# Windowed attention feeding a split-precision SiLU MLP on one core: another order of the weight slices at the MLP's beginning, and the work between token groups put ahead of the rest, with its low parts on VectorE

## Chip, core and metric

One core of a Trainium2 chip runs the whole program in one launch. The metric is the time of one execution on the device in microseconds (us). The profile names the engines PE (TensorE matmuls; PEld are its weight loads), DVE (VectorE), ACT (ScalarE), POOL (GpSimd) and SP (SyncE, from whose queue every DMA of this kernel is issued). Each engine takes its instructions in the order in which the program emits them for it. [...]

## The reference, cut to what matters

```python
# q, k, v: (8 batches, 8 heads, 576 tokens, 64); causal window of 128, ALiBi slopes
scores = q @ k.T / 8 ; scores = where(mask, scores + bias, -1e9)
attn   = softmax(scores) @ v                    # per batch and head
x      = attn.transpose(0, 2, 1, 3).reshape(4608, 512)
h      = x @ w_in                               # w_in (512, 2048)
out    = (h * sigmoid(h)) @ w_out               # w_out (2048, 512), float32
```

## The kernel before, in words

**Tiles.** The 4608 tokens are 36 tiles of 128. Attention works on pairs p = 2i + q (tile i, four of the eight heads each, 72 pairs): `scores` (PE), `row_max` in two halves u (DVE, line 248), `exps` (ACT, 258), `p_hi` (ACT, 267), `p_lo` (DVE, 272), a transposing DMA (280), `attend` (PE, 318), `normalize` in two stages (DVE, 331 to 342), then x split in a high and a low half (ACT 352, DVE 358) and transposed by DMA (375). For each tile the values are split by `v_hi` (POOL, 199) and `v_lo` (DVE, 210). The first eight pairs take another way: transposes on PE (290), high and low parts out of PSUM (ACT 296, DVE 301), and `x_transpose` (PE 367, ACT 368, DVE 369) in four column blocks; their x must be there before the MLP can begin.

**MLP.** Nine groups g of 512 tokens, sixteen slices f of 128 hidden columns. Per slice `gemm1` (line 401, halves 0 and 1 with six products each) makes h in PSUM; then tanh on ACT (`act1`, 408), `act2` on DVE (413), the high part gh on ACT (`act3`, 419) and the low part gl on POOL (`act4`, 424); `gemm2` (436, two halves of six products) adds high*high, high*low and low*high into four PSUM banks. n = 16g + f numbers the slices. At a group's end four banks are stored (`store`, ACT 447 and DVE 445, DMA 448) through two buffers of the tag "io", and xh, xl, which have one buffer, are written for the next group by `x_parts` (ACT 388, POOL 389).

**Weights.** 32 slices ((f, 0) of w_in, (f, 1) of w_out) are loaded through two raw buffers of the tag "big", which the transposed x uses later too, and split in five steps (`w_split1` ACT 465, `w_shift` DVE 471, `w_low` DVE 476, `w_hi` ACT 486, `w_lo` DVE 490) spread over four positions. Some are split ahead of the MLP, the others one at every second position of group 0.

**Order.** All is written out by hand. A position is one half of a gemm; position 0 is the first gemm1 and attention's beginning has negative positions, from -82 on. `put(position, function)` hangs work on a position; `begin()` emits all of a position's work, then the gemm follows; `later(n, ...)` hangs work n positions on. A group has 64 positions: at 58 and 59 of a group stands the last slice's gemm1, at 60 and 61 gemm2 of slice 14, at 62 and 63 gemm2 of slice 15. In each group a pair's `scores` stand at position 58, its two `row_max` at 59 and 60, `v_hi` and `v_lo` of another tile at 60 and 61, and the `attend` that reads this v at 63; the next `scores` stand at 66. PSUM has eight banks: two (tag "a") serve scores, attend and small transposes from position 0 on, two hold h, four hold the outputs. An attend therefore needs a bank that a `row_max` has read, and the next scores need the bank that `normalize` of that attend has read.

The lines on which the prediction's steps rest:

```python
            later(1, act2, n)          # 645 to 647: every slice alike
            later(2, act3, n)
            later(2, act4, n)
            ...
            for i, x in enumerate([("g2", n - 1, 0), ("g2", n - 1, 1), ("g2", n, 0), ("g2", n, 1)]):
                if g + 1 < NG:
                    seq.append(("xt", g + 1, i))     # x_parts of tile i, one ahead of each gemm2 half
                seq.append(x)
```

Of the kernel before, what the change touches and what calls it, by code (L numbers as in the profile page):

```python
# [11 lines left out]
AF = mybir.ActivationFunctionType  # L12
ALU = mybir.AluOpType
# [17 lines left out]
NG = NT // TG  # L31
GT = TG // P
NF = DFF // P
NCC = DM // P
# [15 lines left out]
STEP = 8  # L50
# [2 lines left out]
LAST = [f"{kind}{f}" for f in range(NF - 1, NF - 5, -1) for kind in ("wih", "wil", "woh", "wol")]  # L53
WD = (1, 1, 2, 3)

CLOSE = (-4, 2, 8, 14, 20, 26, 32, 38)
W_EARLY = (-21, -17, -12, -8)


def at(p):  # L60

    if p < 2 * GT:
        return STEP * (p - 2 * GT) - 18
    if p < 4 * GT:
        return CLOSE[p - 2 * GT]
    return STEP * (p - 2 * GT) - LEAD
# [3 lines left out]
def tile_window_attention_then_silu_mlp(ctx, tc, qk, v, w_in, w_out, base8, out):  # L70
    nc = tc.nc
# [29 lines left out]
    xh = const.tile([P, NCC, TG], F32R, name="xh")  # L101
    xl = const.tile([P, NCC, TG], F32R, name="xl")

    def f32(ap):
        return ap.bitcast(F32)
# [4 lines left out]
    def next_tag(use):  # L110
        turn[use] = turn.get(use, -1) + 1
        return bank[use][turn[use] % len(bank[use])]
# [3 lines left out]
    def ps_of(tag, name):  # L116
        t = psum.tile([P, DM], F32, tag=tag, bufs=2 if tag in "ah" else 1, name=name)
        if tag == "a":
            spare["a"] = t
        return t  # L120

    def keep_warm(n):

        for _ in range(n):
            nc.tensor.matmul(
                spare["a"][:, 4 * (D + 1) :], ones16[:, :P], ones16[:, : DM - 4 * (D + 1)],
                start=True, stop=True, skip_group_check=True,
            )
# [52 lines left out]
    def block_of(i):  # L181
        return i % NBLK

    def load_k(i):
        ks[i] = pool.tile([P, NHP, P], F32, tag="k", bufs=KSLOTS, name=f"k{i}")
        nc.sync.dma_start(ks[i], qk[i, 1])

    def load_q(i):
        qs[i] = pool.tile([P, NHP, P], F32, tag="q", bufs=2, name=f"q{i}")
        nc.sync.dma_start(qs[i], qk[i, 0])  # L190
# [132 lines left out]
    xt, whole, now = {}, [], [0]  # L323
# [40 lines left out]
    def x_transpose(cc):  # L364
        xp = ps_of(next_tag("misc"), f"xp{cc}")
        for i in range(GT):
            nc.tensor.transpose(xp[:, i * P : (i + 1) * P], xt[i][:, cc * P : (cc + 1) * P], ident)
        nc.scalar.copy(xh[:, cc], xp)  # L368
        nc.vector.tensor_sub(xl[:, cc], xp, f32(xh[:, cc]))  # L369
# [12 lines left out]
            whole.remove(i)  # L382
            x_dma(i)

    def x_parts(i):
        t, first = xt[i & -2, "t"][:, i % 2], i % GT * P
        cols, scale = slice(first, first + P), vsc[i // NBLK][:, 1:2]
        nc.scalar.activation(xh[:, :, cols], t[:, :NCC], AF.Copy, scale=scale)  # L388
        nc.gpsimd.tensor_scalar(xl[:, :, cols], t[:, NCC:], scale, 1.0, op0=ALU.mult, op1=ALU.mult)  # L389

    hps, gact, ops = {}, {}, {}

# [18 lines left out]
    def act2(n):  # L411
        gt = gact[n]
        nc.vector.scalar_tensor_tensor(out=gt, in0=gt, scalar=1.0, in1=hps[n], op0=ALU.add, op1=ALU.mult)  # L413

    def act3(n):
        gt = gact[n]
        gh = pool.tile([P, TG], F32R, tag="gh", name=f"gh{n}")
        gl = pool.tile([P, TG], F32R, tag="gl", name=f"gl{n}")
        nc.scalar.copy(gh, gt)  # L419
        gact[n] = (gh, gl, gt)  # L420

    def act4(n):
        gh, gl, gt = gact[n]
        nc.gpsimd.tensor_sub(gl, gt, f32(gh))  # L424

    def gemm2(n, half):
        g, f = divmod(n, NF)
# [67 lines left out]
    def put(point, fn, *a):  # L495
        plan.setdefault(max(point, at(0)), []).append((fn, a))

    for p in range(NPAIR):
        i, q = divmod(p, 2)
        n = at(p)  # L500
        a = n + (2 * STEP + 2 if p < 2 * GT else 15 if p < 4 * GT else 13)
        put(n, scores, p)
        if block_of(i) in (SPLIT, SPLIT + 1):
            put(n + 1, other_batch, p)
        put(n + 1, row_max, p, 0)
        put(n + 2, row_max, p, 1)
        put(n + 2, exps, p, 0)
        put(n + 3, exps, p, 1)
        if p < 2 * GT:

            put(n + STEP + 1, p_transpose_first, p, 0)
            put(n + STEP + 1, p_hi_first, p, 0)
            put(n + STEP + 1, p_transpose_first, p, 1)
            put(n + STEP + 1, p_hi_first, p, 1)
            put(n + STEP + 3, p_lo_first, p, 0)
            put(n + STEP + 4, p_lo_first, p, 1)

            put(n + STEP + 1, keep_warm, 4)
            put(n + 2 * STEP + 2, keep_warm, 5)
        else:  # L520
            put(n + 3, p_hi, p, 0)
            put(n + 4, p_lo, p, 0)
            put(n + 4, p_hi, p, 1)
            put(n + 4, p_transpose, p, 0)
            put(n + 5, p_lo, p, 1)
            put(n + 5, p_transpose, p, 1)
        put(a + 0, attend, p)
        z = a + (3 if p < 2 * GT else 1)
        put(z, normalize, p, 0)
        put(z + 1, normalize, p, 1)  # L530
        put(z + 2, x_hi, p)
        put(z + 2, x_lo, p)
        if q == 0:
            if i > 1:
                put(at(2 * i - 3) + 1, load_q, i)
                put(at(2 * i - 3) + 1, load_k, i)
            if i >= GT:
                put(n - 2, load_v, i)
            put(a - 3, v_hi, i)
            put(a - 2, v_lo, i)  # L540
    for b in range(1, NBB):
        n = at(2 * NBLK * b)
# [8 lines left out]
    def later(n, fn, *a):  # L551
        put(pos[0] + n, fn, *a)

    wq = [(f, w) for f in range(NF) for w in range(2)]
    wi = [0, 0, 0]

    def w_next_load():
# [24 lines left out]
    with tc.manual_schedule():  # L582
        nc.gpsimd.memset(ones16, 1.0)
        nc.gpsimd.memset(ones, 1.0)
        make_identity(nc, ident)
        ps_of("a", "warm")
        keep_warm(16)

        warm = const.tile([P, 1], F32, name="warm")
        nc.scalar.activation(warm, ones[:, :1], AF.Exp)  # L590
        load_q(0)
        load_k(0)
        nc.sync.dma_start(tab[:, :, P:], base8[:, :, P:])
        for i in range(VCH):
            vscale_load(0, i)
        load_q(1)
        load_k(1)
        nc.sync.dma_start(tab[:, :, :P], base8[:, :, :P])
        nc.gpsimd.memset(v1[:, :, :, D : D + 1], 1.0)
        for i in range(VCH):  # L600
            put(at(0) + 3 + i // 2, vscale_reduce, 0, i)
        for x in range(3):
            put(at(0) + 8 + x, vscale_finish, 0, x)
        for n in range(2):
            put(at(0) + 14 + 8 * n, w_next_load)
        put(at(0) + 4, keep_warm, 10)
        put(at(0) + 6, keep_warm, 10)
        put(at(0) + 7, keep_warm, 6)
        for n in W_EARLY:
            put(n, w_next)  # L610
        for cc, n in enumerate((23, 24)):
            put(at(2 * GT - 2) + n, x_transpose, cc)
        while pos[0] < 0:
            begin()
            pos[0] += 1
        bank.update(scores=[("a", "a")])

        for g in range(NG):
            now[0] = g

            seq = []
            for f in range(NF):
                n = g * NF + f
                seq += [("g1", n, 0)] + [("xt", 0, 2), ("xt", 0, 3)] * (n == 0) + [("g1", n, 1)]
                if 0 < f < NF - 1:
                    seq += [("g2", n - 1, 0), ("g2", n - 1, 1)]
            n = g * NF + NF - 1
            for i, x in enumerate([("g2", n - 1, 0), ("g2", n - 1, 1), ("g2", n, 0), ("g2", n, 1)]):
                if g + 1 < NG:
                    seq.append(("xt", g + 1, i))  # L630
                seq.append(x)
            for k, n, half in seq:
                if k == "xt":
                    if n == 0:
                        x_transpose(half)
                    else:
                        x_parts(n * GT + half)
                    continue
                begin()
                x_send()  # L640
                if k == "g1":
                    gemm1(n, half)
                    if half == 1:
                        act1(n)
                        later(1, act2, n)
                        later(2, act3, n)
                        later(2, act4, n)
                else:
                    gemm2(n, half)
                    if n % NF == NF - 1:  # L650
                        store(g, 2 * half)
                        store(g, 2 * half + 1)
                if g == 0 and half == 0:
                    w_next()
                pos[0] += 1
        while plan:
            begin()
            pos[0] += 1
# [35 lines left out]
```

## Time and profile before

| what | value |
|---|---|
| median of 3 runs (lowest, highest) | 1046.36 us (1045.06, 1050.79) |
| the profiled execution's own time | 1045.97 us |
| its span, first to last instruction | 1044.2 us |
| busy: PE, DVE, ACT, POOL | 95%, 53%, 44%, 24% of the span |
| mean granted TensorE clock | 0.977 |

The prediction is worked against the profiled execution (1045.97 us). A share of the span says little here: DVE is at 53% on average, but close to full in the first 180 us, in which attention's beginning and all weight slices lie. The rows further down are therefore of single stretches: the beginning (0 to 81 us) and the turns between two groups, which follow each other every 109 us or so.

### The profile page before, as it was taken

How to read it: one execution, taken by the hardware profiler on the slowest of the kernel's cores; microseconds unless marked ns; L12 is line 12 of the kernel's file. 1: busy time of each engine (PE TensorE's matmuls, PEld its weight loads, DVE VectorE, ACT ScalarE, POOL GpSimd, SP SyncE). 2: the span in 40 equal slices, each digit the busy share in tenths (PEclk: the TensorE clock that was granted, in tenths of full speed). 3: DMA queues.
4: the chain of work that ended last, by engine and by line, in shares of the span. 5: the costliest groups of instructions: out<-in, count | busy, mean ns of one | idle time of the engine just before them, and what ended most of it. 6: DMA issues, size and time to landing. Idle time of an engine off the chain costs nothing. (4 is left out here: it accounts for less than half of the span.)

```text
span 1044.2 us, 16900 instructions
## 1 busy us (share of the span) xinstructions
PE 997.2 (95%) x6374; PEld 788.7 (76%) x6374; DVE 555.9 (53%) x1358; ACT 462.3 (44%) x968; POOL 248.5 (24%) x229
## 2 busy tenths in 40 slices
PE   7798898999999999999999999999999999999998
PEld 6676676777777776777777767776777767777886
DVE  5889987455545554545455545544455545542111
ACT  5666667333353445334344454434334454433222
POOL 3012222222222223222222222222222122223221
PEclk8899999999999999999999999999899999999999
DMA  7267977333453445333444445432434443221001
GB/s 232 85 186 191 253 206 191 92 84 78 72 112 81 105 111 139 81 62 81 121 82 81 101 104 131 100 71 65 106 76 74 86 111 79 59 37 51 1 1 40
DMA packets 201072, 104.91 MB, mean 100 GB/s; under 512 B 168224, under 2 KB 176416, under 8 KB 200992
## 3 DMA queue, kind: packets, MB, share of 16 engines
q1 hardware_dynamic: 200992, 103.84, 42.1%
q8 instruction: 50, 0.82, 0.3%
q14 instruction: 30, 0.25, 0.1%
HBM read 54.00 MB, written 9.44 MB: 61 GB/s over the span
## 5 line engine op out<-in xcount | busy, mean ns | idle before, releaser
L424 POOL TENSOR_TENSOR gl<-gt,gh 128x512 fp32r<-128x512 f32 x144 | 186.9, 1298 | 742.2 <-ACT gh L419 575.2
L408 ACT ACTIVATE gt<-h 128x512 f32<-128x512 f32 x144 | 85.9, 597 | 446.7 <-PE h L401 438.0
L436 PE MATMUL o<-woh,gh 128*128 128x512 f32 x576 | 232.4, 404 | 12.4 <-ACT gh L419 12.4
L401 PE MATMUL h<-xh,wih 128*128 128x512 f32 x576 | 238.8, 415 | 2.0 <-ACT xh L368 2.0
L413 DVE SCALAR_TENSOR_TENSOR gt<-gt,h 128x512 f32<-128x512 f32 x144 | 98.9, 686 | 264.8 <-ACT gt L408 264.8
L436 PE MATMUL o<-woh,gl 128*128 128x512 f32 x576 | 232.8, 404 | 5.1 <-POOL gl L424 5.0
L436 PE MATMUL o<-wol,gh 128*128 128x512 f32 x576 | 229.6, 399 | 0.0
L401 PE MATMUL h<-xl,wih 128*128 128x512 f32 x576 | 227.5, 395 | 0.2 <-DVE xl L369 0.2
L401 PE MATMUL h<-xh,wil 128*128 128x512 f32 x576 | 227.6, 395 | 0.0
L272 DVE SCALAR_TENSOR_TENSOR hr<-t,hr 128x512 f16<-128x512 f32 (+1 forms) x128 | 120.8, 944 | 82.8 <-ACT hr L267 82.4
L436 PEld LDWEIGHTS o<-woh,gh 128*128 128x128 f32 x576 | 109.9, 191 | 39.5 <-ACT gh L419 15.5
L436 PEld LDWEIGHTS o<-woh,gl 128*128 128x128 f32 x576 | 109.8, 191 | 36.3 <-POOL gl L424 10.3
L401 PEld LDWEIGHTS h<-xh,wih 128*128 128x128 f32 x576 | 109.0, 189 | 30.0 <-ACT xh L368 2.2
L436 PEld LDWEIGHTS o<-wol,gh 128*128 128x128 f32 x576 | 109.9, 191 | 25.8
L401 PEld LDWEIGHTS h<-xh,wil 128*128 128x128 f32 x576 | 108.8, 189 | 25.1
L401 PEld LDWEIGHTS h<-xl,wih 128*128 128x128 f32 x576 | 109.1, 189 | 20.5 <-DVE xl L369 0.5
L258 ACT ACTIVATE t<-t,mx 128x256 f32<-128x256 f32 (+1 forms) x288 | 120.5, 487 | 9.0 <-DVE mx L248 9.0
L419 ACT CAST gh<-gt 128x512 fp32r<-128x512 f32 x144 | 88.5, 614 | 53.3 <-DVE gt L413 52.4
L248 DVE CUSTOM_DVE_ANT_0 t<-sp,tab 128x256 f32<-128x256 f32 (+1 forms) x288 | 101.0, 404 | 15.2 <-PE sp L228 9.0
L358 DVE TENSOR_TENSOR x<-xs,x 128x256 f16<-128x256 f32 x64 | 73.1, 1143 | 45.5 <-ACT x L352 45.5
L228 PEld LDWEIGHTS sp<-k,q 64*128 64x128 f32 x1088 | 68.9, 192 | 25.7 <-issue 25.0
L228 PE MATMUL sp<-k,q 64*128 64x128 f32 x1088 | 83.4, 291 | 1.4 <-DVE xs L342 1.4
(68 smaller groups left out, 665.6 us busy)
## 6 DMA issues: line engine op xcount, KB each, us to landing
q<-qk SPq DMA_DIRECT2D x36, 256.0 KB, 3.0
k<-qk SPq DMA_DIRECT2D x36, 256.0 KB, 3.2
vm<-v SPq DMA_DIRECT2D x36, 256.0 KB, 3.7
out<-ot SPq DMA_DIRECT2D x36, 256.0 KB, 2.1
wr<-w_in SPq DMA_DIRECT2D x16, 512.0 KB, 3.9
wr<-w_out SPq DMA_DIRECT2D x16, 512.0 KB, 4.0
rv<-v SPq DMA_DIRECT2D x32, 256.0 KB, 3.0
hl<-hr SPq DMA_TRANSPOSE x128, 3.1
```

The source lines that it names most:

```text
L228: nc.tensor.matmul(sp[h][:, u, o], qs[i][rows, 2 * q + u], ks[i - 1 + o][rows, 2 * q + u], start=True, stop=True, skip_group_check=True,)
L248: nc.vector.tensor_tensor_reduce(out=t[:, h, 2 * P - n :], in0=st[p]["sp"][h][:, u, o].rearrange("p o c -> p (o c)"), in1=tab[:, 4 * q + 2 ...
L258: nc.scalar.activation(x, x, AF.Exp, bias=st[p]["mx"][:, 2 * u + h : 2 * u + h + 1], scale=-1.0)
L272: nc.vector.scalar_tensor_tensor(out=hr[:, 1], in0=t[:, :, 2 * P - n :], scalar=PSCALE, in1=hr[:, 0], op0=ALU.mult, op1=ALU.subtract)
L358: nc.vector.tensor_sub(xt[i][:, 1, cols], st[p]["x"], xt[i][:, 0, cols])
L401: nc.tensor.matmul(hps[n], w[:, cc], x, start=(half == 0 and i == 0), stop=(half == 1 and i == len(seq) - 1), skip_group_check=True,)
L408: nc.scalar.activation(gt, hps[n], AF.Tanh, scale=0.5 / W_SCALE)
L413: nc.vector.scalar_tensor_tensor(out=gt, in0=gt, scalar=1.0, in1=hps[n], op0=ALU.add, op1=ALU.mult)
L419: nc.scalar.copy(gh, gt)
L424: nc.gpsimd.tensor_sub(gl, gt, f32(gh))
L436: nc.tensor.matmul(ops[ti], a[:, t], w, start=(f == 0 and i == 0), stop=(f == NF - 1 and i == len(seq) - 1), skip_group_check=True,)
```

## The change

The weight slices come in the sequence (0,0), (1,0), (0,1), (2,0), (1,1), (3,0), (2,1), ... where it was (0,0), (0,1), (1,0), (1,1), ... Three are split ahead of position 0, at positions -72, -19 and -6; before, four were, at -21, -17, -12 and -8. The first two loads stand at -81 and -65, before at -68 and -60. Pair 8's scores move from position -4 to -1, with all that follows from them, its attend staying at 11. Pair 7's attend moves from -8 to -11, ahead of the first `x_transpose`, and loses the filler matmuls (`keep_warm`) in front of it; the other early pairs have theirs behind their attend. At a group's end `turn_over` emits act2, act3 and act4 of the last slice and x_parts of the next group's four tiles at once behind tanh, at position 59; gl of that slice and all xl are DVE's then, not POOL's.

```diff
-CLOSE = (-4, 2, 8, 14, 20, 26, 32, 38)
-W_EARLY = (-21, -17, -12, -8)
+CLOSE = (-1, 2, 8, 14, 20, 26, 32, 38)
...
-    def x_parts(i):
+    def x_parts(i, part):
...
-        nc.scalar.activation(xh[:, :, cols], t[:, :NCC], AF.Copy, scale=scale)
-        nc.gpsimd.tensor_scalar(xl[:, :, cols], t[:, NCC:], scale, 1.0, op0=ALU.mult, op1=ALU.mult)
+        if part == 0:
+            nc.scalar.activation(xh[:, :, cols], t[:, :NCC], AF.Copy, scale=scale)
+            return
+        nc.vector.tensor_scalar(xl[:, :, cols], t[:, NCC:], scale, 1.0, op0=ALU.mult, op1=ALU.mult)
...
-        nc.gpsimd.tensor_sub(gl, gt, f32(gh))
+        (nc.vector if n % NF == NF - 1 else nc.gpsimd).tensor_sub(gl, gt, f32(gh))
+
+    def turn_over(n):
+        i = (n // NF + 1) * GT
+        more = n // NF + 1 < NG
+        if more:
+            x_parts(i, 0)
+        act2(n)
+        act3(n)
+        act4(n)
+        if more:
+            x_parts(i, 1)
+            for k in range(1, GT):
+                x_parts(i + k, 0)
+                x_parts(i + k, 1)
...
-        a = n + (2 * STEP + 2 if p < 2 * GT else 15 if p < 4 * GT else 13)
+        if p == 2 * GT - 1:
+            a = n + 2 * STEP - 1
+        elif p == 2 * GT:
+            a = n + 12
+        else:
+            a = n + (2 * STEP + 2 if p < 2 * GT else 15 if p < 4 * GT else 13)
...
-            put(n + 2 * STEP + 2, keep_warm, 5)
...
-        put(a + 0, attend, p)
+        put(a, attend, p)
+        if p < 2 * GT - 1:
+            put(a, keep_warm, 5)
...
-    wq = [(f, w) for f in range(NF) for w in range(2)]
+    wq = [(0, 0)] + [a for f in range(1, NF) for a in ((f, 0), (f - 1, 1))] + [(NF - 1, 1)]
...
-            put(at(0) + 14 + 8 * n, w_next_load)
+            put(at(0) + 1 + 16 * n, w_next_load)
...
-        for n in W_EARLY:
+        for n in (at(0) + 10, -19, -6):
             put(n, w_next)
...
-            for i, x in enumerate([("g2", n - 1, 0), ("g2", n - 1, 1), ("g2", n, 0), ("g2", n, 1)]):
-                if g + 1 < NG:
-                    seq.append(("xt", g + 1, i))
-                seq.append(x)
+            seq += [("g2", n - 1, 0), ("g2", n - 1, 1), ("g2", n, 0), ("g2", n, 1)]
...
                         act1(n)
-                        later(1, act2, n)
-                        later(2, act3, n)
-                        later(2, act4, n)
+                        if n % NF == NF - 1:
+                            turn_over(n)
+                        else:
+                            later(1, act2, n)
+                            later(2, act3, n)
+                            later(2, act4, n)
```

## Rows read from the trace of the kernel before

**Rows 1.** The view of who waited for whom, PE alone, whole span: the engine, line and tile that waited and what released it; us in total, times, longest us.
```profile
PE o L436 <- ACT gh L419: 12.4, 7, 1.8
PE av L318 <- DVE mx L248: 9.1, 6, 3.0
PE xp L367 <- DVE x L342: 5.2, 1, 5.2
PE o L436 <- POOL gl L424: 5.0, 10, 0.6
```

**Rows 2.** The view by stretches (windows): a stretch, its length, busy us of each engine (PE, PEld, DVE, ACT, POOL) with the number of instructions, the granted TensorE clock, DMA share, GB/s. The second and the third turn between groups.
```profile
288.00:298.00 10.00, 7.58 (x47) 5.41 (x46) 3.57 (x5) 6.65 (x13) 3.67 (x5) 0.83 0.39 113
398.00:408.00 10.00, 7.58 (x53) 5.51 (x52) 3.83 (x6) 7.46 (x16) 3.87 (x5) 1.00 0.48 123
```

**Rows 3.** The timeline of PE at four turns (first 177, second 287, third 397, sixth 724): start us, us, instruction; in brackets the idle time before it and what ended it. In each turn the first row is the first product of gemm2 of slice 14 and the last row the scores at position 66; of the second turn also the first product of slice 15's gemm2.
```profile
177.21 0.40 PE L436 MATMUL o<-woh,gh 128*128 128x512 f32 x1
...
191.49 0.72 PE L228 MATMUL sp<-k,q 64*128 64x128 f32 x8
...
286.99 0.40 PE L436 MATMUL o<-woh,gh 128*128 128x512 f32 x1
...
291.75 0.50 PE L436 MATMUL o<-woh,gh 128*128 128x512 f32 x1 [1.79 <-ACT gh L419]
...
300.52 1.16 PE L228 MATMUL sp<-k,q 64*128 64x128 f32 x16
...
397.19 0.40 PE L436 MATMUL o<-woh,gh 128*128 128x512 f32 x1
...
409.38 1.19 PE L228 MATMUL sp<-k,q 64*128 64x128 f32 x16
...
724.31 0.40 PE L436 MATMUL o<-woh,gh 128*128 128x512 f32 x1
...
739.21 1.16 PE L228 MATMUL sp<-k,q 64*128 64x128 f32 x16
```

**Rows 4.** The timeline of ACT at the second turn: tanh, xh of the first tile, two exps, p_hi, gh.
```profile
287.25 0.60 ACT L408 ACTIVATE gt<-h 128x512 f32<-128x512 f32 x1 [4.61 <-PE h L401]
287.75 0.72 ACT L388 ACTIVATE xh<-xt,vsc 128x512 fp32r<-128x512 f16 x1
288.36 0.90 ACT L258 ACTIVATE t<-t,mx 128x256 f32<-128x256 f32 x2
...
290.57 0.62 ACT L267 ACTIVATE hr<-t 128x512 f16<-128x512 f32 x1
291.09 0.61 ACT L419 CAST gh<-gt 128x512 fp32r<-128x512 f32 x1
```

**Rows 5.** The timeline of DVE at the second turn: act2, v_lo, the last of the four stores, normalize's second stage.
```profile
287.88 0.69 DVE L413 SCALAR_TENSOR_TENSOR gt<-gt,h 128x512 f32<-128x512 f32 x1 [2.22 <-ACT gt L408]
288.49 1.10 DVE L210 SCALAR_TENSOR_TENSOR v<-rv,vsc,v 128x512 f16<-128x512 f32 x1
...
298.17 0.69 DVE L445 TENSOR_SCALAR ot<-o 128x512 f32<-128x512 f32 x1 [1.66 <-DMA out<-ot]
...
299.18 0.42 DVE L342 TENSOR_TENSOR xs<-av,r 128x256 f32<-128x256 f32 x1
```

**Rows 6.** Groups of instructions by line and shape, whole span: busy us, mean ns of one, idle time before them. The low part of a w_in slice; row_max over 256 columns.
```profile
L490 DVE TENSOR_TENSOR wil<-wm,wih 128x512 fp32r<-128x512 f32 x16 | 11.9, 741 | 1.5 <-ACT wih L486 1.4
L248 DVE CUSTOM_DVE_ANT_0 t<-sp,tab 128x256 f32<-128x256 f32 x256 | 93.6, 419 | 8.5 <-PE sp L228 8.5
```

**Rows 7.** The page's list of DMA issues: how many, KB each, median us from issue to landing.
```profile
out<-ot SPq DMA_DIRECT2D x36, 256.0 KB, 2.1
xt<-x SPq DMA_TRANSPOSE x32, 3.1
```

**Rows 8.** The timeline of SP ahead of the first turn: the four transposing DMAs of the next group's x.
```profile
171.77 5.49 SPq L375 DMA_TRANSPOSE xt<-x  x4
```

**Rows 9.** The timeline of DVE at the beginning: the first weight slice's shift; the low parts of pair 7; normalize of pair 7; the memset with which pair 8 begins; the two gaps behind it; the row_max that frees the bank for the attend at position 11.
```profile
40.46 0.43 DVE L471 TENSOR_SCALAR wm<-wm 128x512 int32<-128x512 int32 x1 [0.23 <-ACT wm L465]
...
44.90 1.28 DVE L301 SCALAR_TENSOR_TENSOR hl<-pt,hl 128x512 f16<-128x512 f32 x2
...
53.74 0.22 DVE L331 TENSOR_SCALAR r<-av,vsc 128x4 f32<-128x4 f32 x1 [0.78 <-PE av L318]
...
55.86 0.79 DVE L239 MEMSET sp<- 64x384 f32 x2 [0.78 <-PE sp L228]
...
59.27 0.69 DVE L272 SCALAR_TENSOR_TENSOR hr<-t,hr 128x512 f16<-128x512 f32 x1 [1.26 <-ACT hr L267]
60.80 1.29 DVE L369 TENSOR_TENSOR xl<-xp,xh 128x512 fp32r<-128x512 f32 x2 [0.84 <-ACT xh L368]
...
80.42 0.42 DVE L248 CUSTOM_DVE_ANT_0 t<-sp,tab 128x256 f32<-128x256 f32 x1
```

**Rows 10.** The timeline of PE at the beginning: the attend at position 11.
```profile
80.99 1.46 PE L318 MATMUL av<-v,hl 128*128 128x65 f16 x24 [2.96 <-DVE mx L248]
```

**Rows 11.** The timeline of ACT at the beginning: the second half of pair 1's exps.
```profile
15.35 0.69 ACT L258 ACTIVATE t<-t,mx 128x128 f32<-128x128 f32 x2 [0.76 <-DVE mx L248]
```

**Rows 12.** The view of the raw weights' tile, up to 40 us, in which two slices are loaded while the first inputs still come in: us from issue to landing.
```profile
DMA to landing us min/median/max: 6.7/7.0/7.3
```

**Rows 13.** Groups of instructions by line and shape, whole span: a store on DVE, which reads PSUM.
```profile
L445 DVE TENSOR_SCALAR ot<-o 128x512 f32<-128x512 f32 x18 | 12.4, 692 | 45.5 <-PE o L436 33.3 <-DMA out<-ot 12.2
```

More of the change, by code (lines that the diff above doesn't have):

```diff
@@ L608, in tile_window_attention_then_silu_mlp @@
         put(at(0) + 7, keep_warm, 6)
-        for n in W_EARLY:
+        for n in (at(0) + 10, -19, -6):
             put(n, w_next)
-        for cc, n in enumerate((23, 24)):
-            put(at(2 * GT - 2) + n, x_transpose, cc)
+        for cc in range(2):
+            put(at(2 * GT - 2) + 23 + cc, x_transpose, cc)
         while pos[0] < 0:
@@ L627, in tile_window_attention_then_silu_mlp @@
             n = g * NF + NF - 1
-            for i, x in enumerate([("g2", n - 1, 0), ("g2", n - 1, 1), ("g2", n, 0), ("g2", n, 1)]):
-                if g + 1 < NG:
-                    seq.append(("xt", g + 1, i))
-                seq.append(x)
+            seq += [("g2", n - 1, 0), ("g2", n - 1, 1), ("g2", n, 0), ("g2", n, 1)]
             for k, n, half in seq:
                 if k == "xt":
[L634 to L637, printed above, removed]
+                    x_transpose(half)
                     continue
```

## Prediction

> **What bounds the kernel now.** I read first who waits for whom on PE, since PE is busy nearly all the time: what it waits for is what can be won. Four entries carry nearly all of it [rows 1]: gh at seven places, row_max ahead of an attend (the two PSUM banks of tag "a"), once 5.2 us for pair 6's x, and gl at ten places. The stretches then show where: the seven gh waits stand one at each turn between groups, and the clock counts too. [...] From the first product of slice 14's gemm2 to the scores at position 66 the first turn takes 14.28 us, the second 13.53, the third 12.19, the sixth 14.90 [rows 3]. [...] I let the second stand for the fourth, fifth and seventh too; six turns are then 81.2 us. Within a turn PE does twelve products in 2.8 us: (291.75 - 1.79 - 0.40 - 286.99) / 11 = 0.234 each [rows 3].
>
> Why gh is late: tanh ends at 287.85, act2 at 288.57, but ACT does an xh, exps, an xh, exps and a p_hi before gh at 291.09 [rows 4, 5].
>
> **The turn after the change.** Zero is the first product of slice 14's gemm2. tanh 0.26 to 0.86, act2 0.89 to 1.58, gh right behind it 1.6 to 2.2 (xh of the first tile fits beside act2) [rows 4, 5]; gl on DVE like the low part of a weight, 0.74 [rows 6], 2.25 to 3.0. PE wants gh at 2.8 and gl two products later, 3.27: both waits go.
>
> What is late next stands behind gl in DVE's queue. Position 59 now emits act2, gl and four xl ahead of position 60's row_max and 61's v_lo; before, row_max came in front of act2, and v_lo right behind it. The attend at 63 needs both, v_lo for its values and row_max for its bank. An xl is a tensor_scalar from SBUF to SBUF of 512 columns; the trace has none on DVE. Its ends are the shift of a weight slice, 0.43 [rows 9], and a store out of PSUM, 0.69 [rows 13]; it is like the first in both its places, so I take 0.43 and keep 0.69 for the range. A next instruction starts 0.08 before the end of the one in front (288.49 against 287.88 + 0.69 [rows 5]): four xl take 1.4 and end at 4.3, row_max two of 0.42 [rows 6], at 0.35 each, 5.0. v_lo is between 0.69 (act2's size) and 1.10 (its row, beside POOL's work [rows 5]); POOL has nothing there in the new order, so I take 0.8. attend starts at 5.8. PE is ready for it after eighteen products, at 4.2: a new wait of 1.6.
>
> [...]
>
> From 5.8 PE needs 0.73 for the attend (half of 1.46 at the lower clock [rows 10]), 1.4 for six products and 2.8 for twelve: ready for the scores at 10.75. These need the bank that normalize frees, and normalize stands behind the last store, which waits for a store's DMA [rows 5]. That chain: ACT does three more xh behind gh (0.62 each), to 4.05, then exps to 4.8, the second exps from row_max's first result on to 5.7, p_hi to 6.25 (durations [rows 4]); p_lo 0.69 to 6.95. SP's queue has p_lo's transposing DMA in front of the stores: 1.37 for one issue (5.49 / 4 [rows 8]), 8.3; the second store's issue at 8.7 (0.4 for the first, my estimate); landed 2.1 later [rows 7], 10.85; last store and normalize take 1.43 (298.17 to 299.60 [rows 5]). Scores at 12.4. So the turn ends by the stores, not by PE, and the wait of 1.6 ahead of the attend is inside it, as is a fall of the clock behind that wait. A fall behind the second wait (10.75 to 12.4) would show: 1.34 (13.53 - 12.19 [rows 3]), one turn in four or five, 0.3 each; bounds 0 and 2.7.
>
> Six turns: 6 × 12.4 + 1.8 = 76.2 against 81.2: **-5.0**.
>
> **The first turn** differs. One slice fewer is split early, so the last one starts at 56, not 54, and x can be sent only at 59, not 57. On SP the four transposing DMAs then stand behind q and k of pair 20, which wait for the scores of 58. These end at -2.8; with 1.0 for q and k (estimate) x issues at -1.8, the fourth at 2.3 [rows 8], landed at 5.4 [rows 7]; its xl, row_max 6.5, then the small reduction for which a transpose on PE waits at 62, and exps, p_hi, p_lo to 9.1, transposing DMA 10.45, stores landed 13, scores at 14.4 against 14.28 [rows 3]; with a chance of a slow stretch **+0.6** (-1 to +3).
>
> **The last turn** has no attention and the last slice no x: gl on DVE comes in time. They have two of the ten gl waits, none over 0.6 [rows 1]: **-0.8**.
>
> **The beginning.** Before, DVE splits two slices from 40.46 on, and pair 7's low parts begin at 44.90 [rows 9]; pair 6's normalize stands behind them, which is PE's 5.2 us [rows 1]. After, only slice (1,0) is there: low parts at 42.9, pair 6's x at 45.0. attend of pair 7 now goes first, waiting some 2 us for these low parts. Then two blocks of x, each transposes 0.5, xh 0.6, xl 0.7 and handovers, 2.05 together; not overlapped, because pair 7's attend keeps one of the two banks until a normalize that stands behind both. That normalize begins at 49.2 instead of 53.74: 4.5 earlier. Behind it slice (0,1) costs 2.4 on DVE and ACT, so pair 8's memset comes at 52.4 instead of 55.86: 3.5 earlier. From it to the row_max at 80.42 DVE has the same instructions in another sequence, and 2.1 us of gaps [rows 9], of which I take 1.3 as closed, because other work now stands where they are. PE waits 2.96 us for this row_max [rows 10]; its own way there shortens more than DVE's, so DVE sets the end: 4.8 earlier. Weights: a w_out slice now has 6 positions from split to use, as each w_in slice had before, and no low part of a weight is in the list of PE's waits: 0; if that cover were gone, it would be DVE's next instruction that is waited for anyway.
>
> Slice (0,0) at -72 stands in front of pair 1's second exps in ACT's queue. Its load, issued near 9.8 behind the first inputs, takes about 6.7 [rows 12]: landed at 16.5, against exps at 15.35 [rows 11]. That delays DVE and ACT by up to 1.8; the filler matmuls on PE hide most: 0.3 taken. On SP its load goes ahead of q and k of tile 2, which pair 4 is the first to read: 0. Fillers behind the attend instead of in front: 0. Sum **-4.5** (bounds -7.5 and 0).
>
> From position 11 to 56 each position has what it had, one slice shifted: 0.
>
> **Sum:** -4.5 - 5.0 + 0.6 - 0.8 = -9.7 on 1045.97, 1036.3. The median of the runs is 0.4 above that execution, so 1036.5.
>
> [...]
>
> **Rivals.** *The stores don't bind*: if normalize is through by 10.75, only the attend's wait is left, and six turns take 64.5: -16.7, in all 1025. For it: SP's issues may be quicker than I add them up. Against: the last store waits for a DMA already now [rows 5]. 12%.
> *Slow low parts*: xl at 0.69 moves the chain by 1.0 to 13.4, the turns then lose 1.0 with their slow stretches: 1042.7. 12%.
> *A beginning without gain*: the early slice holds pair 1's exps for its full 1.8 and PE carries it on, and DVE, which is full from 40 to 81, eats the rest: 1041. 14%.
> *Slower*: the clock. [...] 8%.
>
> **Numbers.** Forecast 54%, its own range 1031 to 1042; most of it and the first rival are faster by over 0.5% (5.2 us, about what a measurement of this kernel tells from no change), of the third rival half: 70%. Within 0.5%: 22%. Slower: the clock, 8%. The range 1025 to 1044 leaves out the clock rival and half of the first.
>
> **What would show it.** Right: no gh wait and no gl wait at seven turns; in their place waits of about 1.6 of attends for DVE (row_max or v_lo) at six, a short wait of scores for normalize; xl near 0.43; no wait of 5.2 for pair 6's x; attend of position 11 near 76 us behind a longer wait. Wrong: attends at the turns without a wait, or turns above 13.5 us, or the attend of position 11 where it was.

## The result, and the profile after

The changed kernel takes 1052.13 us (median; 1046.22 to 1057.94) against 1046.84 (1041.60 to 1051.00): a ratio of 1.0055, 95% interval 1.0031 to 1.0079, so 3 to 8 us slower where 10 faster was forecast. Its profiled execution is the slowest of its runs, 1057.94 us (span 1056.1, granted clock 0.973); the stage sums below come from it and overstate the loss by the clock, by about 6 us.

Against the span of before it is 11.9 longer. By the starts on PE: -0.5 up to the first product of slice 14's gemm2 at the first turn (176.74 against 177.21); +2.9 in the first turn; +10.9 in the six others; -1.4 in the last turn and the last slice, where the waits for gl went.

The view of who waited for whom, PE alone (us in total, times, longest), answers to [rows 1]:

```profile
PE sp L227 <- DVE xs L341: 14.6, 7, 3.5
PE av L317 <- DVE mx L247: 13.2, 12, 2.9
PE vt L162 <- DVE vcol L158: 8.3, 2, 4.7
PE av L317 <- DVE v L209: 3.8, 6, 0.6
PE o L452 <- POOL gl L425: 1.8, 2, 1.5
```

The seven waits for gh are gone, as are those for gl at the turns. In their place stand scores waiting for normalize, and attends for row_max and then v_lo. PE's timeline at the first, second and third turn (start, us; in brackets the idle time before it) answers to [rows 3]:

```profile
176.74 0.40 PE L452 MATMUL o<-woh,gh 128*128 128x512 f32 x1
...
184.42 0.37 PE L162 MATMUL vt<-ident,vcol 128*1 128x128 f32 x1 [4.72 <-DVE vcol L158]
...
289.42 0.40 PE L452 MATMUL o<-woh,gh 128*128 128x512 f32 x1
...
294.45 0.28 PE L317 MATMUL av<-v,hl 128*128 128x65 f16 x4 [0.67 <-DVE mx L247]
295.37 0.76 PE L317 MATMUL av<-v,hl 128*128 128x64 f16 x20 [0.64 <-DVE v L209]
...
300.26 0.48 PE L227 MATMUL sp<-k,q 64*128 64x128 f32 x2
302.72 2.04 PE L227 MATMUL sp<-k,q 64*128 64x128 f32 x14 [1.97 <-DVE xs L341]
...
318.99 1.16 PE L227 MATMUL sp<-k,q 64*128 64x128 f32 x16
...
402.44 0.40 PE L452 MATMUL o<-woh,gh 128*128 128x512 f32 x1
...
417.33 1.13 PE L227 MATMUL sp<-k,q 64*128 64x128 f32 x14 [3.51 <-DVE xs L341]
```

At the second turn two scores fit into a free bank at 300.26, 10.84 from zero (the forecast had PE ready at 10.75); the others run at 302.72, 13.30 from zero. From there to the next scores at 318.99 it is 16.3, where before it was always 13.2. The stretches of the second turn (engines PE, PEld, DVE, ACT, POOL, then the clock) answer to [rows 2] and say why:

```profile
297.00:300.00 3.00, 3.00 (x15) 2.41 (x13) 0.69 (x2) 0.00 (x0) 0.00 (x0) 1.00 0.83 211
300.00:303.00 3.00, 1.03 (x6) 0.61 (x6) 1.36 (x4) 1.48 (x3) 0.00 (x0) 0.93 0.96 264
303.00:306.00 3.00, 3.00 (x17) 2.58 (x17) 2.46 (x9) 0.63 (x2) 1.15 (x1) 0.50 0.50 139
306.00:309.00 3.00, 3.00 (x8) 2.32 (x8) 0.68 (x4) 0.00 (x0) 0.13 (x1) 0.50 0.00 0
```

Taken in stretches of 1 us, the granted clock stands at 1.00 (986 of the first 1043 before, 987 of 1056 now) or at 0.50 (37 and 49), and between the two only where it changes. Through the attend's two waits it holds at 1.00 (293 to 297 us), and behind the wait of the scores it falls to 0.50. The turns of before lost clock too: besides the second, at 0.83 in [rows 2], the fourth to the seventh, whose stretches in the trace of before are these (columns as above):

```profile
506.00:516.00 10.00, 7.59 (x47) 5.41 (x46) 3.69 (x5) 6.67 (x14) 3.81 (x5) 0.83 0.37 105
616.00:626.00 10.00, 7.98 (x48) 5.48 (x47) 3.69 (x5) 7.72 (x16) 4.13 (x6) 0.83 0.47 146
725.00:735.00 10.00, 7.66 (x43) 5.46 (x42) 3.69 (x5) 6.37 (x13) 3.98 (x6) 0.73 0.38 110
837.00:847.00 10.00, 7.58 (x45) 5.39 (x45) 3.46 (x5) 6.54 (x13) 3.55 (x5) 0.83 0.37 101
```

So five of its six turns fell, and only the third kept 1.00. In the changed kernel it is again five of six: 0.50 from 303, 419, 528, 641 and 750 us on, and 1.00 from 847 to 870, at the seventh. DVE at the second turn of the changed kernel, answering to [rows 5]:

```profile
291.68 0.69 DVE L425 TENSOR_TENSOR gl<-gt,gh 128x512 fp32r<-128x512 f32 x1 [0.69 <-ACT gh L420]
292.29 1.67 DVE L390 TENSOR_SCALAR xl<-xt,vsc 128x512 fp32r<-128x512 f16 x4
...
294.56 0.75 DVE L209 SCALAR_TENSOR_TENSOR v<-rv,vsc,v 128x512 f16<-128x512 f32 x1
...
301.14 0.69 DVE L461 TENSOR_SCALAR ot<-o 128x512 f32<-128x512 f32 x1 [3.45 <-DMA out<-ot]
...
302.15 0.42 DVE L341 TENSOR_TENSOR xs<-av,r 128x256 f32<-128x256 f32 x1
```

The last store waits 3.45 for the DMA of the second one, which has the same buffer, and normalize stands behind it. SP, answering to [rows 8], the first turn's x and the second turn's p_lo and first two stores:

```profile
174.89 6.20 SPq L374 DMA_TRANSPOSE xt<-x  x4
...
296.52 1.23 SPq L279 DMA_TRANSPOSE hl<-hr  x1
297.84 1.01 SPq L464 DMA_DIRECT2D out<-ot  x2
```

The first turn has a wait of its own: x is sent from 174.89 on (171.77 before), the last xl on DVE is late by it, and row_max and the small reduction stand behind that xl. PE waits 4.72 for the reduction, the row at 184.42 above; from 184 to 190 us the granted clock is 0.50 to 0.51.

In the beginning, ACT (first) and DVE (second) answer to [rows 11] and [rows 9]:

```profile
17.07 0.67 ACT L481 ACTIVATE wm<-wr 128x512 f32<-128x512 f32 x1 [2.23 <-DMA wr<-w_in]
17.65 0.68 ACT L257 ACTIVATE t<-t,mx 128x128 f32<-128x128 f32 x2
```

```profile
18.24 1.49 DVE L492 SCALAR_TENSOR_TENSOR wm<-wr,wm 128x512 int32<-128x512 int32 x1
...
44.54 0.43 DVE L487 TENSOR_SCALAR wm<-wm 128x512 int32<-128x512 int32 x1 [0.25 <-ACT wm L481]
...
57.09 0.78 DVE L238 MEMSET sp<- 64x384 f32 x2 [0.15 <-issue]
...
80.08 0.42 DVE L247 CUSTOM_DVE_ANT_0 t<-sp,tab 128x256 f32<-128x256 f32 x1
```

Slice (0,0)'s split waits 2.23 for its load, and pair 1's second exps come at 17.65 (15.35 before). The first shift behind the early pairs comes 4.1 late; the row_max at 80.08 is 0.3 early, and with it the attend at position 11, at 80.66 on PE where it was 80.99 [rows 10]. From 20 to 26 us the granted clock was 1.00 before and 0.50 after (the stretches 12 to 20 and 20 to 26, before, then after):

```profile
12.00:20.00 8.00, 5.12 (x32) 4.28 (x33) 5.49 (x28) 4.15 (x15) 3.81 (x5) 0.57 0.86 277
20.00:26.00 6.00, 6.00 (x84) 5.54 (x82) 5.01 (x21) 3.76 (x10) 3.58 (x5) 1.00 0.30 89
```

```profile
12.00:20.00 8.00, 3.55 (x21) 2.65 (x21) 5.20 (x20) 3.71 (x12) 3.56 (x4) 0.53 0.88 273
20.00:26.00 6.00, 5.79 (x42) 4.72 (x43) 4.47 (x18) 2.76 (x7) 4.87 (x6) 0.50 0.31 90
```

### The profile page after: what moved, and what is told of

Its sections match the earlier page's. It is cut to its first block, busy times and chain, and to the rows that moved or that the text cites. A ratio compares the mean times of both kernels' runs of the same rounds, so it can differ in the third digit from the quotient of the medians.

```text
span 1056.1 us, 16874 instructions
## 1 busy us (share of the span) xinstructions
PE 1002.5 (95%) x6369; PEld 794.9 (75%) x6369; DVE 574.5 (54%) x1399; ACT 463.3 (44%) x968; POOL 219.0 (21%) x188
## 4 chain that ended last, share of the span: by engine, by line
PE 79%; DVE 9%; DMA 5%; ACT 3%; issue 3%; SPq 1%; POOL 0%; DVEq 0%; ACTq 0%; POOLq 0%
PE h L402 35%; PE o L452 32%; PE sp L227 7%; PE av L317 4%; DMA wr<-w_in 2%; DMA out<-ot 2%; DVE wm L492 1%; DVE xl L390 1%; DVE wm L487 1%; DVE hr L271 1%; DVE ot L461 1%; DMA vm<-v 1%; DVE t L247 1%; ACT t L257 1%; DVE gt L414 1%
## 5 line engine op out<-in xcount | busy, mean ns | idle before, releaser
L425 POOL TENSOR_TENSOR gl<-gt,gh 128x512 fp32r<-128x512 f32 x135 | 176.9, 1310 | 800.0 <-ACT gh L420 643.3
L402 PE MATMUL h<-xh,wih 128*128 128x512 f32 x576 | 242.6, 421 | 0.2 <-ACT xh L367 0.2
L402 PE MATMUL h<-xl,wih 128*128 128x512 f32 x576 | 230.6, 400 | 0.5 <-DVE xl L368 0.5
L452 PE MATMUL o<-woh,gl 128*128 128x512 f32 x576 | 229.3, 398 | 1.8 <-POOL gl L425 1.8
L402 PE MATMUL h<-xh,wil 128*128 128x512 f32 x576 | 230.3, 400 | 0.0
L271 DVE SCALAR_TENSOR_TENSOR hr<-t,hr 128x512 f16<-128x512 f32 (+1 forms) x128 | 121.1, 946 | 74.8 <-ACT hr L266 74.4
L402 PEld LDWEIGHTS h<-xh,wih 128*128 128x128 f32 x576 | 110.9, 193 | 29.1 <-issue 1.2
L452 PEld LDWEIGHTS o<-woh,gl 128*128 128x128 f32 x576 | 108.7, 189 | 28.8 <-POOL gl L425 2.9
L452 PEld LDWEIGHTS o<-woh,gh 128*128 128x128 f32 x576 | 109.1, 189 | 25.4 <-ACT gh L420 0.5
L227 PEld LDWEIGHTS sp<-k,q 64*128 64x128 f32 x1088 | 74.2, 199 | 41.2 <-issue 40.9
L227 PE MATMUL sp<-k,q 64*128 64x128 f32 x1088 | 89.9, 300 | 14.7 <-DVE xs L341 14.6
```

The costliest lines, as they stand in the source:

```text
L227: nc.tensor.matmul(sp[h][:, u, o], qs[i][rows, 2 * q + u], ks[i - 1 + o][rows, 2 * q + u], start=True, stop=True, skip_group_check=True,)
L271: nc.vector.scalar_tensor_tensor(out=hr[:, 1], in0=t[:, :, 2 * P - n :], scalar=PSCALE, in1=hr[:, 0], op0=ALU.mult, op1=ALU.subtract)
L402: nc.tensor.matmul(hps[n], w[:, cc], x, start=(half == 0 and i == 0), stop=(half == 1 and i == len(seq) - 1), skip_group_check=True,)
L425: (nc.vector if n % NF == NF - 1 else nc.gpsimd).tensor_sub(gl, gt, f32(gh))
L452: nc.tensor.matmul(ops[ti], a[:, t], w, start=(f == 0 and i == 0), stop=(f == NF - 1 and i == len(seq) - 1), skip_group_check=True,)
```

## The experiments

The theory after the result: *the loss is the turn's. The scores wait behind a store that waits for a DMA, and PE's idle wait is followed by a stretch at a granted clock of 0.50; the beginning gains some us and gives them back.* The rivals: the loss is the beginning's; the attend's waits are what costs; the clock falls for another reason than the wait; and the turns of before lose as much clock, so that only the later scores are left as the loss. The table gives, from the traces, the time from the first product of slice 14's gemm2 to the next pair's scores (position 74), for the first turn and turns two to seven.

| run | median, ratio to before (95%) | first | two to seven | sum of six |
|---|---|---|---|---|
| before | 1046.84 | 27.5 | 26.7 25.5 26.9 26.4 28.1 27.0 | 160.6 |
| changed | 1052.13, 1.0055 | 30.4 | 29.6 29.7 28.1 28.1 29.7 26.4 | 171.5 |
| start_only | 1045.90, 0.9994 (0.9970 to 1.0019) | 28.8 | 26.7 25.5 27.0 25.4 27.0 25.4 | 157.1 |
| turn_only | 1050.39, 1.0051 (1.0024 to 1.0077) | 27.3 | 26.5 29.1 29.5 26.5 29.7 26.4 | 167.8 |
| early_later | 1049.59, 1.0021 (0.9994 to 1.0048) | 30.4 | 29.6 27.3 26.4 28.1 28.4 28.0 | 167.8 |
| stores_late | 1037.15, 0.9913 (0.9888 to 0.9938) | 30.2 | 24.4 28.2 24.4 27.7 24.3 24.3 | 153.4 |
| xl_behind_v | 1055.98, 1.0087 (1.0057 to 1.0117) | 28.7 | 27.9 29.7 29.3 29.3 27.9 27.8 | 171.9 |
| both_moves | 1034.10, 0.9883 (0.9855 to 0.9912) | 27.2 | 24.2 27.8 24.3 27.7 24.2 24.2 | 152.4 |
| fillers_in_h | 1047.92, 1.0008 (0.9989 to 1.0028) | 31.6 | 26.5 27.8 26.4 26.5 26.4 26.4 | 160.1 |
| four_buffers | 1033.18, 0.9875 (0.9846 to 0.9904) | 30.1 | 24.1 28.5 24.3 24.1 24.1 24.1 | 149.1 |
| four_buffers_xl_behind | 1025.57, 0.9807 (0.9781 to 0.9832) | 26.7 | 23.3 29.0 23.5 23.2 23.2 23.2 | 145.3 |
| same_old_start | 1026.80, 0.9815 (0.9788 to 0.9842) | 24.3 | 23.2 28.3 23.2 23.3 23.2 23.2 | 144.5 |

**Half of the change alone.** `start_only` has the changed beginning and the turn of before; `turn_only` the other way round (the diff is the change's own, cut at the turn).

> Only the beginning of the change (order of the slices, early split of slice (0,0), pair 8 and pair 7 moved), turns between groups as before. Theory: the early slice's ACT step waits 2.2 us for its load ahead of pair 1's exps, and the lower clock lasts longer behind it, so all starts some 4 us late and the 4 us won between 40 and 81 us are eaten: first shift of a slice on DVE near 44.5 us, first product of slice 14's gemm2 within 1 us of 177; in all 1046 to 1049. Rival, the predicted one: the beginning gives 4.5, 1042.

> Only the turn of the change (x_parts, act2 to act4 at once, gl and xl on DVE), beginning as before. Theory: PE is ready for the scores at 10.8 us from the first product of slice 14's gemm2, they wait to 13.3 for normalize behind the last store, and the clock falls behind this wait: next scores at 28 to 29.6 instead of 25.5 to 28.1; the whole loss lies here: 1050 to 1054. Rival: the loss is the beginning's and the turns are level or gain 5: 1042 to 1047.

The turn alone is as slow as the whole change, 1.0051 against 1.0055; the beginning alone gives nothing that can be told. The rival that the beginning is the loss falls. In start_only the first product at the first turn came at 173.9, not within 1 us of 177: the beginning had gained 3.3 there, and the first turn took 1.3 of it back.

**The early slice.**

```diff
-        for n in (at(0) + 10, -19, -6):
+        for n in (-58, -19, -6):
```

> The changed kernel, with slice (0,0) split at position -58 instead of -72, where its load has long landed. Theory: no wait of ACT for this load, pair 1's exps near 15.4 us again, shorter stretch at the lower clock, DVE's first shift of the next slice near 40.5 to 42: 2.5 to 4 us less than the changed kernel, 1048 to 1050. Rival: the low clock of the beginning comes from the sequence of the work and not from this wait, then nothing moves: 1052.

The wait for the load is gone and the clock is back at 1.00 from 20 to 26 us, yet the first shift came at 42.49: better than 44.54, not the 40.46 of before. So moving the slice wins back half in this run. That the rest is what its split costs DVE and ACT there (DVE is busy 13.7 of the 15 us from 26 to 41 before) is argued, not shown: in both_and_start, with the slice at the same place, the shift came at 41.65, and in the three runs with the old beginning at 40.46 to 41.74. The two ratios overlap, so for the whole time this is no more than a hint.

**The stores.** The last two stores of a group behind normalize:

```diff
+                        if half == 1 and g + 1 < NG:
+                            later(2, store, g, 2)
+                            later(2, store, g, 3)
+                        else:
                             store(g, 2 * half)
                             store(g, 2 * half + 1)
```

> The changed kernel, with the last two stores of a group emitted two positions later, behind normalize (last group as it was). Theory: normalize no longer stands behind a store that waits for an earlier store's DMA; scores at 11 us instead of 13.3, no fall of the clock behind them: at six turns 2 us of wait and 1.5 to 3 of clock each in the profiled run, half of the clock's in the median: some 15 us less than the changed kernel, 1035 to 1040. Rival: another thing of the chain (p_lo's DMA, the store's bank, tanh behind the store on ACT) keeps PE waiting as long, or the attend's wait alone lets the clock fall: 1048 to 1052.

15 us less than the changed kernel. DVE at the second turn: normalize (L332 to L341) goes ahead, and the store waits alone:

```profile
297.00 0.43 DVE L341 TENSOR_TENSOR xs<-av,r 128x256 f32<-128x256 f32 x1
300.10 0.69 DVE L461 TENSOR_SCALAR ot<-o 128x512 f32<-128x512 f32 x1 [2.67 <-DMA out<-ot]
```

The attend's waits are all still there (0.67 and 0.63), and at four of six turns the clock kept 1.00. The two turns of 28.2 and 27.7 have a further wait in the first gemm2, 1.34 and 0.90 for gh.

**xl behind row_max and v_lo.** The mirror image: the attend's waits removed, the stores as changed.

```diff
-            x_parts(i, 1)
             for k in range(1, GT):
                 x_parts(i + k, 0)
-                x_parts(i + k, 1)
+            for k in range(GT):
+                later(2, x_parts, i + k, 1)
```

> The changed kernel, with the four xl emitted two positions later, behind row_max and v_lo in DVE's queue; stores as in the changed kernel. Theory: the attend at 63 no longer waits (4.2 instead of 5.0 and 5.9), but the scores still stand behind the store's DMA, 13 to 13.3, now after a longer idle wait of some 3.3: no gain, the clock falls at as many turns or more: 1050 to 1056. The first turn's wait of 4.7 for the small reduction goes with it and gives up to 3. Rival: the attend's wait is what costs, 1.3 and the clock at each turn: 1038 to 1042.

> The changed kernel with both moves: last two stores behind normalize, xl behind row_max and v_lo. Theory: neither wait is left, scores near 9.6 from the first product of slice 14's gemm2, next scores near 22.8 to 23, at every turn and without a low clock, against 24.3 with 1 or 2 falls in six in the run with the late stores alone; first turn shorter by 2 to 4: 1022 to 1030. Rival: p_lo or gemm1 then waits for xl and the gain of the second move is lost: 1035 to 1038.

Alone it is no gain (1.0087 against 1.0055, with intervals that overlap): PE comes earlier to the same scores and waits longer (second turn):

```profile
291.41 0.92 PE L317 MATMUL av<-v,hl 128*128 128x65 f16 x24
...
300.33 1.13 PE L227 MATMUL sp<-k,q 64*128 64x128 f32 x14 [3.39 <-DVE xs L341]
```

The clock fell at all six turns: behind these scores the products start 0.43 apart for a while, 0.23 further on. The rival that the attend's wait is what costs falls with it. With both moves the scores run at 9.3, but only 0.1 to 0.2 of it is left at the next scores: the second move's gain was lost, as that run's rival had it, though not by p_lo or gemm1 waiting for xl. What is late is on ACT: its third store stands ahead of tanh, as in the changed kernel, and waits for a store's DMA, so that tanh, act2 and gh of the next slices are late for a PE that now comes earlier (ACT, second turn):

```profile
295.43 0.60 ACT L463 ACTIVATE ot<-o 128x512 f32<-128x512 f32 x1 [3.53 <-DMA out<-ot]
...
297.94 0.62 ACT L420 CAST gh<-gt 128x512 fp32r<-128x512 f32 x1 [1.13 <-DVE gt L414]
```

**Fillers.** Is it the wait itself that the clock falls behind? Sixteen matmuls ahead of the scores, nothing else changed.

> The changed kernel, with 16 filler matmuls (252 columns, results unused) put on PE directly ahead of the scores at position 66 of each turn; the wait for normalize stays as it is, but PE is not idle in most of it. Theory (the clock falls behind the idle wait): scores at 13.3 from the first product of slice 14's gemm2 as before, but the next scores at 26.4 at nearly every turn instead of 28 to 29.7: 5 to 10 less than the changed kernel, 1042 to 1047. Rival: the clock falls for another reason (the attend's wait, or chance), or the fillers push the scores back: 1051 to 1056.

This run told nothing of the clock: fillers into attend's bank waited for normalize like the scores (6 waits, 15.1 us) and came on top, 1064.47 (1.0170). Written into the bank of the next gemm1 they wait for nothing:

```diff
+                if 0 < g and pos[0] % (4 * NF) == 2:
+                    hps[n] = psum.tile([P, TG], F32, tag="h", bufs=2, name=f"h{n}")
+                    for _ in range(16):
+                        nc.tensor.matmul(hps[n][:, : 2 * P], ones16[:, :P], ones16, ...)
```

> The changed kernel, with 16 filler matmuls (256 columns, 0.107 us each at the upper clock, results overwritten) ahead of the scores at position 66 of each turn, written into the PSUM bank that the next slice's gemm1 takes anyway, so that they wait for nothing that the scores wait for; in the earlier run with fillers they used the bank of attend, waited for normalize themselves and came on top. Theory (the clock falls behind PE's idle wait): scores at 13.3 to 13.6 from the first product of slice 14's gemm2 as in the changed kernel, next scores at 26.4 at nearly all turns instead of 28 to 29.7: 5 to 10 less than the changed kernel, 1042 to 1047. Rival: the clock falls without the idle time too, 1051 to 1054.

The scores run at 13.3 as in the changed kernel (14.6 at the third turn), with 0.24 of idle time instead of 1.97, and the clock stays (PE at the second turn; the stretches of the second turn to be held against those above):

```profile
300.09 1.92 PE L658 MATMUL h<-ones 128*128 128x256 bf16 x16
...
302.66 1.13 PE L227 MATMUL sp<-k,q 64*128 64x128 f32 x14 [0.24 <-DVE xs L341]
```

```profile
303.00:306.00 3.00, 3.00 (x24) 2.49 (x21) 2.82 (x11) 0.62 (x1) 1.20 (x1) 1.00 0.40 133
306.00:309.00 3.00, 3.00 (x15) 2.42 (x14) 1.00 (x3) 2.21 (x6) 0.10 (x1) 1.00 0.02 5
```

Useless work thus makes the kernel some 4 us faster (1.0008 against 1.0055), 11.4 in the six turns of the profiled runs, and none of these six lost clock (the first turn did, ahead of its fillers). That is what the clock behind this wait costs the changed kernel, shown by itself.

It is not the change's loss against before. With no clock lost in its six turns the filled kernel is only level with before, which lost clock at five of them: five of its turns take 26.4 to 26.5, where the turns of before that kept the clock take 25.4 to 25.5 (before, start_only). The granted clocks of all runs agree: their median is 0.979 over the 16 runs of the changed kernel and 0.977 over 33 of the one before. The clock is a cost that both kernels pay; what the change adds is mainly that the scores start later.

**Four buffers.** The stores through the four buffers of x, free at a turn, instead of two; nothing reordered. Then the same with xl behind, and the best of these with the old beginning.

```diff
-        tag, bufs = ("x", 4) if g == NG - 1 else ("io", 2)
+        tag, bufs = "x", 4
```

> The changed kernel, order untouched, with the four stores of every group through the four buffers of x, which are free at a turn, instead of two of io. Theory: the third and fourth store no longer wait for a DMA, normalize comes right behind them, scores at 10.8 without a wait, next scores near 24 to 24.4: as good as the late stores or a little better, 1033 to 1038. Rival: the scores wait for p_lo and its DMA in SP's queue or for x_hi behind a store: 1046 to 1052.

> As the run with four buffers, and the four xl behind row_max and v_lo. Theory: PE is not held at all at a turn, scores at 9.3, and since no store waits on ACT, gh of the next slices is in time too, which the run with both moves lost: next scores at 22.5 to 23.2 instead of 24.2; 1024 to 1031. Rival: x_hi waits on ACT for a store's DMA and gh is late again, next scores at 24: 1032 to 1036.

> As the run with four buffers and xl behind, with the beginning of the kernel before. It differs from that run in the beginning alone, with turns that hold no long wait. Theory: what the new order of slices gains from 40 to 81 us the early slice eats before that, and the first turn, whose x is sent two positions later, loses again: 0 to 2.5 slower than the run with the new beginning. Rival, the predicted beginning: 4 slower.

The times of all three came out as the theory had them. In four_buffers the order of the work is the changed kernel's, so its 19 us are what the waits for the stores' buffers cost, clock included. 1025.57 (0.9807) is the fastest kernel here, and the one with the old beginning is level with it. At the second turn of the fastest, PE has no wait ahead of attend or scores:

```profile
287.53 0.92 PE L317 MATMUL av<-v,hl 128*128 128x65 f16 x24
292.58 1.48 PE L227 MATMUL sp<-k,q 64*128 64x128 f32 x16
```

Only the third turn stays long, 28 to 29, in each of these runs. In the fastest one ACT waits 3.57 there for a DMA of the next batch's values, with gh behind it; that was not tried further.

**Two slices more, earlier.** Both moves, slice (0,0) at -58, and two extra splits at positions 33 and 45.

> Both moves, slice (0,0) split at position -58, and two more splits in group 0 (positions 33 and 45), so that the last slice is done four positions earlier and the first turn's x can be sent at 55 to 57. Theory: the first turn's x is there in time, so the first turn is as short as the others (next scores at 23 to 25 instead of 30), and the beginning is 1 to 3 shorter: 1016 to 1026. Rival: the two extra splits crowd DVE, which is over 90% busy there, and PE waits in group 0 for what the turn gains: as with both moves alone, 1022 to 1030.

1041.14 (0.9943, 0.9922 to 0.9965), worse than the moves alone. The first turn fell to 24.8 as meant, but ahead of it the extra splits held normalize on DVE, and one pair's scores waited 4.35 for it at 159 us.

## Why the prediction was wrong

**What held.** gh and gl came in time, and the waits moved where they were forecast: attend behind four xl, scores behind the last store. xl took 0.42 each (1.67 for four; 0.43 was taken, the shift's [rows 9]), v_lo 0.75 without POOL beside it (0.8). The attend, put at 0.73 as half of the 1.46 that it took at a clock of 0.54 ([rows 10]; 80.9 to 82.5 us), takes 0.75 from its start to the next product where it is in one piece at a clock of 1.00 (four_buffers_xl_behind, 287.53 to 288.28). PE was ready for the scores at 10.84 (10.75).

**The step that failed** is the end of the turn: "Scores at 12.4", with "A fall behind the second wait" priced at "one turn in four or five, 0.3 each". Two parts. The chain came to 13.30 instead of 12.4: p_lo's DMA was issued on time (8.33 against 8.3), but the second store's issue was through at 9.4, not 8.7, and its DMA took longer than 2.1, so that its buffer was free at 11.7, not 10.85; at the third turn, where a load of values lies beside it, the scores ran at 14.89. The six turns' scores come to 81.6, all at a clock of 1.00, where 74.4 without the clock was forecast. Before they came to 81.2, but only 73.1 of that (six times the 12.19 of the third turn) is without the clock, and 8.1 is clock. Then the clock: in the profiled run it took 10.8 behind the scores in six turns, where 1.8 was forecast. So of the 10.9 that the six turns lost against before, some 8.5 is later scores and only 2.7 more clock (the rest is -0.3). PE's waits at the second turn add up to 3.28 (0.67, 0.64, 1.97) where they were 2.42 (1.79, 0.63): the change traded the wait for gh, behind which the clock fell at five of six turns, for longer ones, behind which it fell at five of six again.

**Why it was priced so low.** The third turn of before kept a clock of 1.00 [rows 2] with waits of 1.79 and 0.63, and I took that as evidence that such waits are mostly free. The prediction's own figures said otherwise: 81.2 for six turns against 73.1 at the third's 12.19 is 1.35 of clock a turn, where the new turn was given 0.3. The range given for it, 0 to 2.7 (14.90 - 12.19 [rows 3]), held the 1.6 of three turns but not the 3.1 and 2.9 of two others; the error was to take a tenth of it. The rival named for this, the clock, had 8%, and the median is 1052.1, slower as that rival had it. But of the two new waits only the scores' was followed by 0.50, at five of the six turns, and the attend's (0.67 and 0.64) at none; the chain was 0.9 longer than forecast; and of the 4.5 of the beginning 0.5 came.

**The beginning**, -4.5. In the pair of profiles 0.5 came, and the attend at position 11, forecast near 76, stayed where it was: 80.66, a sign that the prediction had named for being wrong. Over the profiled runs the first product of slice 14's gemm2 stands at 173.9 to 176.7 with the changed beginning and the slice at -72 (nine runs, mean 175.4), at 177.2 to 179.7 with the old one (three runs, mean 178.6): about 3 gained. From pair 7's low parts on DVE went as forecast (46.99 to 80.08, 33.1 us, where 42.9 to 75.6 was forecast); the failed term is slice (0,0), "0.3 taken", where its wait and split put the first shift at 43.2 to 44.5 in those nine runs against 40.5 to 41.7. Filler matmuls on PE did not hide it; that DVE, not PE, carries the early pairs is the likely reason, but no run tests it.

**The first turn**, +0.6: +2.9 in the profiled run, and 2.4 with turns otherwise clean (26.7 against 24.3). The chain there was foreseen to a us (row_max through at 7.4, forecast 6.5), but the 4.72 on PE ahead of the reduction's transpose, and the clock of 0.50 to 0.51 behind it, were not priced. Together the beginning and the first turn give nothing that can be told: start_only 0.9994, and same_old_start within 1.2 us of its twin. **The last turn**, -0.8: -1.4.

## What to carry to other kernels

When a change moves a wait, price the old and the new one with their clock: look at the stretch behind every wait of that length in the trace, and take a wait that was followed by a clock of 1.00 once as no proof. An engine that issues a store in front of work that others need should not be waiting for that store's buffer; two more buffers, with nothing reordered, gave 19 us here (four_buffers against the changed kernel), where putting the turn's work earlier had lost 5. And test a suspected clock loss by filling the wait with useless matmuls that depend on nothing the wait depends on, and set what comes back against the clock that the old kernel loses too.

## What the runs showed of the hardware

Waits of 0.66 to 0.82 and of 0.64, one us apart, were not followed by a granted clock of 0.50 in any of the nine turns of stores_late and four_buffers that had no wait for gh behind them. The wait of 1.8 to 2.1 for gh, with one of 0.2 to 0.6 for gl behind it, was followed by it in 8 of 12 turns (before, start_only). The scores' wait of 1.9 to 2.4 was followed by it in 10 of 15 (changed, turn_only, early_later), their wait of 2.75 to 3.51 at the third turn of these runs in two of three, and their wait of 3.3 to 4.5 (xl_behind_v) in six of six. How long the stretch at 0.50 lasts varies from turn to turn in one execution (next scores 1.6 late, or 2.8 to 3.1). This is likely most of why 16 executions of the changed kernel spread over 12 us: 12 with the wait filled (fillers_in_h) spread over 3.4, and 6 of four_buffers_xl_behind over 1.4. In the changed kernel's trace w_low took 1.49 at 18.24 and 1.75 at 173.46, POOL at work both times, and 0.69 at 166.63, with POOL idle.
